# Softmax chain, score-gradient chain and contractions at top priority, and part of the ending moved from VectorE and GpSimd to GpSimd and SyncE

## The chip, the cores and the metric

The kernel runs on one core of one Trainium2 chip. The metric is the device time of one execution in microseconds (us). A core has TensorE (matmuls, "PE" in the profile; its weight loads are "PEld"), VectorE ("DVE"), ScalarE ("ACT"), GpSimd ("POOL") and SyncE ("SP"), which here only issues transfers. The transfers run on 16 DMA engines. Transfers issued by SyncE and by GpSimd stand in two different queues of the profile.

Executions of one kernel spread by 1 to 2% here (the kernel before: 497.7 to 502.1 us in one round of tests, 494.1 to 501.7 in another). A run over 1.5% above the fastest of the same kernel counts as slow and is left out of every ratio.

## The reference

One layer, forward and backward. Two batches, one query each, 32 query heads over 16 heads of keys and values, 4096 keys, head size 128, model size 576, and a bilinear MLP of width 4608:

```python
def _fwd_reference(A_x, A_k_cache, A_v_cache, A_wq, A_wo, B_x, B_w_gate, B_w_up, B_w_down):
    # ... cut: _A_ref is the attention, _B_ref the MLP
    x = A_x
    xn = _layernorm(x, axis=-1)
    return x + _A_ref(xn, A_k_cache, A_v_cache, A_wq, A_wo) + _B_ref(xn, B_w_gate, B_w_up, B_w_down)

def reference(A_x, A_k_cache, A_v_cache, A_wq, A_wo, B_w_gate, B_w_up, B_w_down, B_x, grad_out):
    # ... cut: f is the forward pass of the arguments
    _out, _vjp = jax.vjp(_f, A_x, A_k_cache, A_v_cache, A_wq, A_wo, B_w_gate, B_w_up, B_w_down)
    _grads = _vjp(grad_out)
    return (_out, *_grads)
```

The outputs include the gradients of keys and values, as large as the caches: 92.48 MB are read and 92.48 MB written. There is little arithmetic per byte.

## The kernel before

The attention is cut into 16 steps. A step takes two heads of keys and values of one batch. It transposes K on VectorE and computes scores on TensorE, runs the softmax chain, does the same pass over V for the gradient of the probabilities, and runs the score-gradient chain. The contraction of V with the probabilities (`end_of_V`) closes the step; the contraction of K with the score gradients (`end_of_K`) comes in the next one. The gradients of K and V are outer products: TensorE writes pairs of PSUM banks, ScalarE casts them to bf16, and GpSimd issues stores of 1 MB. Nine of the steps (0, 1, 2, 5, 6, 9, 10, 13, 14) carry a unit of the MLP beside all this.

TensorE, VectorE and ScalarE run their instructions in the order in which the kernel was built. That order is chosen by a scheduler from the written order, from priorities, and from when a buffer can be free.

The two kinds of block that matter below:

```python
    def contract(rowsT, heads):
        o_ps = ps_m([P, Dh])
        with Block() as mm:                     # 64 matmuls, each on 32 of the array's columns
            for c4 in range(4):
                for c8 in range(8):
                    for x, head in enumerate(heads):
                        cg = 2 * x + c8 % 2
                        mm(o_ps[32 * cg:32 * cg + 32, :], lhsT=..., rhs=head[:, 8 * c4 + c8, :], ...)
        # ... cut: copy to SBUF and one small matmul

    def head_scores(n, t, x, s_ps, half):
        # ... cut: one VectorE transposition of a quarter of K or V
        with Block() as mm:                     # 16 matmuls on all 128 columns
            for e in range(2):
                for c8 in range(8):
                    mm(s_ps[:, ...], lhsT=view(X[:], ...), rhs=view(W[t][:], ...), ...)
```

The chain of the softmax, with what each of its small results needs in PSUM:

```python
    def ps_m(shape, dtype=FP32):                # the two "general" PSUM buffers
        return ps.tile(list(shape), dtype, tag="m", bufs=2, name="ps_m")

    def softmax(s_ps):
        s_ps = by_rows(s_ps)
        mx = small("mx")
        nc.vector.reduce_max(mx[:], s_ps[:], axis=AX.X)
        mT = ps_m([1, P])                       # general buffer
        nc.tensor.transpose(mT[:], mx[:], identf[:])
        # ... cut: maximum of mT, then a matmul into a general buffer, then negb on VectorE
        nc.scalar.activation(ex[:], s_ps[:], AF.Exp, bias=negb[:], scale=SCALE, accum_out=z[:])
        z_ps = ps_m([P, 1])                     # general buffer
        # ... cut: probabilities pr, their transposition pT
```

The contractions, the MLP and the small products of the score-gradient chain use the same two general buffers. All banks of PSUM are taken: 2 general, 2 for scores, 2 pairs for outer products, 8 in all.

The main loop and the ending:

```python
    for n in range(NIT):                        # 16 steps
        # ... cut: pass over K, with end_of_K of the step before
        pr, pT, ex, rz = softmax(s_ps)
        prm = masked(pr, "prm")
        # ... cut: pass over V, first part of the next MLP unit
        ds, dsT = dscores(pr, ex, rz, dp_ps)
        dsm = masked(ds, "dsm")
        end_of_V(st, b, s, V, pT)
    # ending: last outer products, gradients of wq and wo of the last group, gradient of x
```

Of the kernel before, what the change touches and what calls it, by code (L numbers as in the profile page):

```python
# [13 lines left out]
P = 128  # L14
# [9 lines left out]
def kernel(  # L24
# [653 lines left out]
    def back_units(st):  # L678
        g, wq, wo, oT = st["g"], st["wq"], st["wo"], st["oT"]
        n0 = g * GH * Dh  # L680
        m = {}
        stq = nat if g == NGRP - 1 else swtile

        def first():
            yp = ps_m([P, 5, 2])
# [25 lines left out]
        def outer_q(k, A):  # L711
            def f():
                R = m["R"]
                if A == 0:
                    m["st"] = stq([P, 2, GH * P], "stq")
                st = m["st"]
                o, whole = ps_pair()
                with Block() as mm:
                    for dc in range(2):
                        for aa in range(2):  # L720
                            a = 2 * A + aa
                            d0 = (2 * k + dc) * P
                            mm(o[aa][:, 256 * dc:256 * dc + 256], lhsT=xnr[32 * a:32 * a + 32, d0:d0 + P],
                                             rhs=R[32 * a:32 * a + 32, 1].rearrange("p h d -> p (h d)"),
                                             start=True, stop=True)
                evac_pair(lambda aa: view(st[:], 0, P, 512 * A + 256 * (aa or 0),
                                          ([[256, 2]] if aa is None else []) + [[GH * P, 2], [1, 256]]), o, whole, 1024,
                          lambda x: x.rearrange("p a (d n) -> p a d n" if whole is not None else "p (d n) -> p d n", d=2))
                if A == 1:
                    nc.gpsimd.dma_start(out_4[256 * k:256 * k + 256, n0:n0 + GH * P].rearrange("(c p) n -> p c n", p=P),  # L730
                                        st[:])
            return f

        def outer_qt():
            R = m["R"]
            st = tailtile("stqt")
            for A in range(2):
                o = ps_o()
                with Block() as mm:
                    for aa in range(2):  # L740
                        a = 2 * A + aa
                        mm(o[64 * A:64 * A + 64, aa, 0:256], lhsT=xnr[32 * a:32 * a + 32, 512:576],
                                         rhs=R[32 * a:32 * a + 32, 1].rearrange("p h d -> p (h d)"), start=True, stop=True)
                evac(st[64 * A:64 * A + 64].rearrange("p (a n) -> p a n", a=2), o[64 * A:64 * A + 64, :, 0:256], 512)
                nc.gpsimd.dma_start(out_4[512:576, n0 + 512 * A:n0 + 512 * A + 512], st[64 * A:64 * A + 64])

        def outer_o(A, h2, k):
            def f():
# [12 lines left out]
                          lambda x: x[:, :, 0:HD2] if whole is not None else x[:, 0:HD2])  # L761
                if h2 == 1 and k == 1:
                    r0 = n0 + 4 * A * P
                    nc.gpsimd.dma_start(out_5[r0:r0 + 4 * P, :].rearrange("(h p) n -> p h n", p=P), m["so"][:])
            return f

        return [[first], [second], [outer_o(0, 0, 0), outer_o(0, 0, 1)], [outer_o(0, 1, 0), outer_o(0, 1, 1)],
# [25 lines left out]
        return n  # L793

    def end_of_K(st, b, s, K, dsT):
        t_ps = contract(dsT, K)
        nc.vector.tensor_scalar(st["oT"][:, 1, 4 * s:4 * s + 4, b], t_ps[:], SCALE, None, op0=ALU.mult)
        dve(0.2)

    def end_of_V(st, b, s, V, pT):  # L800
        t_ps = contract(pT, V)
        nc.vector.tensor_copy(st["oT"][:, 0, 4 * s:4 * s + 4, b], t_ps[:])
        dve(0.2)

# [8 lines left out]
    def final_units():  # L813
# [40 lines left out]
        def gradient():  # L854
            rowf, xn_f, dy_f = m["rowf"], m["xn"], m["dy"]
            dxn = rowf[:, 1, :]
            m1 = fin([2, 1], FP32, "m1")
            nc.vector.reduce_sum(m1[:], dxn, axis=AX.X)
            nc.vector.tensor_scalar(m1[:], m1[:], 1.0 / D, None, op0=ALU.mult)
            xs2 = fin([2, D], FP32, "xs2")  # L860
            m2 = fin([2, 1], FP32, "m2")
            nc.vector.tensor_tensor_reduce(
                out=xs2[:], in0=dxn, in1=xn_f[:], scale=1.0 / D, scalar=0.0,
                op0=ALU.mult, op1=ALU.add, accum_out=m2[:],
            )
            t1 = fin([2, D], FP32, "t1")
            nc.vector.tensor_scalar(t1[:], dxn, m1[:], None, op0=ALU.subtract)
            t3 = fin([2, D], FP32, "t3")
            nc.vector.tensor_scalar(t3[:], xn_f[:], m2[:], None, op0=ALU.mult)
            nc.vector.tensor_sub(t1[:], t1[:], t3[:])  # L870
            nc.vector.tensor_scalar(t1[:], t1[:], rstd[:], None, op0=ALU.mult)
            dx_bf = fin([2, D], BF16, "dx_bf")
            nc.vector.tensor_add(dx_bf[:], t1[:], dy_f[:])
            nc.sync.dma_start(out_1.rearrange("b s d -> (b s) d"), dx_bf[:])

        return [[prepare], [output], [rows], [gradient]]
# [10 lines left out]
    for n in range(NIT):  # L887
# [9 lines left out]
        for x in range(2):  # L897
            K.append(slot(kview, 0, b, l0 + x, s_ps, per, (lambda: end_of_K(*last[:5])) if x == 0 and last else None))
            if x == 0:
# [3 lines left out]
                        side[0:0] = back_units(last[0])  # L903
                        per = -(-len(side) // 4)
                bd1 = build_bd(st, b, s, 1)
        pr, pT, ex, rz = softmax(s_ps)
        prm = masked(pr, "prm")
        if n + 1 < NIT and not new:
            build_W(st, *step(n + 1)[1:], 0)
# [10 lines left out]
                    build_W(nxt, 0, 0, 0)  # L920
        if n + 1 < NIT:
            build_W(nxt if new else st, *step(n + 1)[1:], 1)
        ds, dsT = dscores(pr, ex, rz, dp_ps)
        dsm = masked(ds, "dsm")
        end_of_V(st, b, s, V, pT)
        last = (st, b, s, K, dsT, dsm, bd0)
# [42 lines left out]
```

## Time and profile before

| | before |
|---|---|
| time, median of 3 runs | 500.26 us (498.81 to 502.59) |
| span of the profiled run | 496.4 us |
| moved | 186.06 MB |
| last load landed | 435.5 us |
| from there to the end | 60.9 us |
| last ScalarE cast ended | 489.2 us |

And from the table of stretches, the stretch up to the landing of the last load and the rest (busy us with counts for PE, PEld, DVE, ACT and POOL, then granted TensorE clock, DMA share, GB/s):

```profile
0.00:435.50 435.50, 338.46 (x6671) 235.09 (x6737) 292.28 (x605) 306.46 (x383) 232.13 (x371) 0.91 1.00 391
435.50:496.40 60.90, 40.76 (x675) 22.28 (x680) 34.89 (x76) 41.98 (x57) 31.95 (x34) 0.89 0.71 262
```

While loads still arrive the transfers are always at work and reach 391 GB/s on average; the rest, stores only, goes at 262 GB/s.

### The profile page before, as it was taken

Reading aid. Unit: us, or ns where it says so; the run is one execution under the profiler, and the core shown is the slowest. Engines: PE = TensorE matmul, PEld = TensorE weight load, DVE = VectorE, ACT = ScalarE, POOL = GpSimd, SP = SyncE. Lnnn points to the kernel's source line nnn. Section 1 sums busy time; section 2 is a strip of 40 time slices with the busy share of each in tenths; the row PEclk is TensorE's granted clock in tenths of the full one; section 3 lists DMA queues with packets and bytes.
Section 4 is the critical chain, followed back from the end, with each engine's and each line's share of the span. In section 5 each row is a group of like instructions: output and inputs, shape, how many; then the busy total and the mean of one; then the engine's idle time right before and its main releaser. Section 6 shows DMA issues by size and latency. Waiting matters only on the chain.

```text
span 496.4 us, 16989 instructions
## 1 busy us (share of the span) xinstructions
PE 379.2 (76%) x7344; PEld 257.4 (52%) x7417; DVE 327.2 (66%) x680; ACT 348.4 (70%) x439; POOL 264.1 (53%) x404
## 2 busy tenths in 40 slices
PE   2676887876868877788997768669888869888943
PEld 1655665553645555565665446446556537564510
DVE  6786795861848675855887465666778474884483
ACT  4143877867747857877986768749876777899833
POOL 3245365762634646675546346538647346487613
PEclk9875999988968989989999879969999798999995
DMA  8998999999899999999999999999999999996765
GB/s 256 384 394 304 378 415 390 422 421 407 303 393 356 407 414 360 419 419 412 401 422 407 417 421 346 413 372 353 409 420 411 417 418 372 415 372 240 264 260 190
DMA packets 52899, 186.06 MB, mean 375 GB/s; under 512 B 4140, under 2 KB 19128, under 8 KB 44632
## 3 DMA queue, kind: packets, MB, share of 16 engines
q1 hardware_dynamic: 28392, 92.49, 48.4%
q0 software_dynamic: 24432, 92.48, 47.1%
q8 instruction: 58, 0.95, 0.7%
q14 instruction: 17, 0.14, 0.1%
HBM read 92.48 MB, written 92.48 MB: 373 GB/s over the span
## 4 chain that ended last, share of the span: by engine, by line
DMA 34%; PE 25%; ACT 12%; DVE 11%; issue 7%; POOL 5%; POOLq 0%; ACTq 0%; DVEq 0%
DMA out_dram<-so 22%; PE ps_o L105 10%; ACT so L124 10%; DMA kv<-in_A_k_cache_dram 7%; PE ps_m L105 7%; DVE X L141 6%; DMA kv<-in_A_v_cache_dram 5%; PE ps_sc L105 4%; POOL bd L532 2%; ACT std L124 1%; DVE Xw L141 1%; POOL prm L597 1%; PE ps_m L591 1%; DVE dense L529 1%; ACT sto L124 0%
## 5 line engine op out<-in xcount | busy, mean ns | idle before, releaser
L124 ACT CAST so<-ps_o 128x1024 bf16<-128x1024 f32 x249 | 238.6, 1021 | 70.3 <-PE ps_o L105 29.1
L141 DVE STREAM_TRANSPOSE X<-kv 128x1024 f32<-128x1024 f32 x128 | 157.4, 1232 | 41.2 <-DMA kv<-in_A_k_cache_dram 13.6
L105 PEld LDWEIGHTS <-X 128*128 128x128 bf16 x2048 | 81.9, 103 | 36.6 <-DVE X L141 19.6
L105 PE MATMUL ps_sc<-W,X 128*128 128x64 bf16 (+1 forms) x2048 | 90.1, 200 | 12.1 <-DVE X L141 9.9
L618 POOL DMA_DIRECT2D out_dram<-so x64 | 50.0, 782 | 71.0 <-ACT so L124 43.0
L105 PE MATMUL ps_o<-bd,dsm 128*128 128x512 bf16 x219 | 74.4, 414 | 11.7 <-ACT so L124 8.7
L105 PE MATMUL ps_o<-bd,prm 128*128 128x512 bf16 x212 | 69.0, 396 | 13.8 <-ACT so L124 6.1
L532 POOL TENSOR_TENSOR bd<-dense,maskq 128x1024 bf16<-128x1024 bf16 x32 | 60.6, 1892 | 17.3 <-DVE dense L529 16.1
L124 ACT CAST stw<-ps_o 128x1024 bf16<-128x1024 f32 x36 | 34.4, 1019 | 15.6 <-PE ps_o L105 12.0
L124 ACT CAST std<-ps_o 128x576 bf16<-128x576 f32 x36 | 21.3, 648 | 27.7 <-PE ps_o L105 22.9
L514 POOL COPY W<-rep 32x16 bf16<-32x16 bf16 x128 | 25.0, 195 | 27.0 <-PE ps_sc L105 19.2
L105 PE MATMUL ps_m<-kv,rowT 128*32 128x128 bf16 x2048 | 37.5, 228 | 2.0 <-issue 1.7
L105 PEld LDWEIGHTS <-dsm 128*128 128x128 bf16 x256 | 22.2, 105 | 29.9 <-issue 22.8
L597 POOL TENSOR_TENSOR prm<-pr,maskc 128x1024 bf16<-128x1024 bf16 x16 | 30.2, 1889 | 13.5 <-DVE pr L648 12.8
L105 PEld LDWEIGHTS <-prm 128*128 128x128 bf16 x256 | 21.1, 101 | 28.8 <-issue 15.6
L105 PEld LDWEIGHTS <-rowT 128*32 128x32 bf16 x2048 | 31.1, 101 | 6.9 <-issue 4.4
L597 POOL TENSOR_TENSOR dsm<-ds,maskc 128x1024 bf16<-128x1024 bf16 x16 | 30.4, 1900 | 5.8 <-DVE ds L669 5.5
L124 ACT CAST sto<-ps_o 128x576 bf16<-128x576 f32 x27 | 16.5, 650 | 14.1 <-PE ps_o L105 12.8
L141 DVE STREAM_TRANSPOSE Xw<-wgu 128x1152 f32<-128x1152 f32 x18 | 24.2, 1352 | 2.4 <-PE ps_sc L105 2.4
L105 PEld LDWEIGHTS <-Wdy 128*128 128x128 bf16 x306 | 20.7, 103 | 9.0 <-issue 3.2
L105 PEld LDWEIGHTS <-xnr 32*128 32x128 bf16 (+1 forms) x440 | 13.0, 98 | 19.9 <-issue 15.1
L414 POOL DMA_DIRECT2D out_dram<-stw x18 | 13.9, 771 | 14.4 <-ACT stw L124 14.3
(186 smaller groups left out, 550.5 us busy)
## 6 DMA issues: line engine op xcount, KB each, us to landing
out_dram<-so POOLq DMA_DIRECT2D x64, 1024.0 KB, 13.1
kv<-in_A_k_cache_dram SPq DMA_DIRECT2D x32, 1024.0 KB, 13.0
kv<-in_A_v_cache_dram SPq DMA_DIRECT2D x32, 1024.0 KB, 16.2
out_dram<-stw POOLq DMA_DIRECT2D x18, 512.0 KB, 12.2
wd<-in_B_w_down_dram SPq DMA_DIRECT2D x9, 576.0 KB, 8.1
out_dram<-std POOLq DMA_DIRECT2D x9, 576.0 KB, 10.3
wo<-in_A_wo_dram SPq DMA_DIRECT2D x4, 1152.0 KB, 11.4
wgu<-in_B_w_gate_dram SPq DMA_DIRECT2D x9, 512.0 KB, 14.9
```

What stands on the lines that cost most here:

```text
L105: ins = nc.tensor.matmul(*args, **kwargs)
L124: nc.scalar.copy(out, in_)
L141: nc.vector.transpose(out, in_)
L414: nc.gpsimd.dma_start(out[0:512, f0:f0 + FS].rearrange("(c p) n -> p c n", p=P), st[:])
L514: nc.gpsimd.tensor_copy(view(W[t][:], 32 * a, 32, 48 + 4 * a, [[2 * WW, 4], [WW + 2, 2], [1, 2]]), view(st["rep"][:], 32 * a, 32, t * 4 * ...
L529: nc.vector.tensor_copy(dense[:], bp[:])
L532: nc.gpsimd.tensor_tensor(bd[:], view(dense[:], 0, P, 0, [[Dh, 2], [0, 4], [1, Dh]]), view(maskq[:], 0, P, 0, [[0, 2], [1, 4], [0, Dh]]), ...
L591: nc.tensor.matmul(t_ps[:], lhsT=o_sb[:], rhs=RV[:].rearrange("p x r -> p (x r)"), start=True, stop=True)
L597: nc.gpsimd.tensor_tensor(m[:], view(rows[:], 0, P, 0, [[0, 8], [1, P]]), view(maskc[:], 0, P, 0, [[1, 8], [0, P]]), ALU.mult)
L618: nc.gpsimd.dma_start(oview[b, :, :, l0 + x].rearrange("a m n -> m a n"), st[:].rearrange("p a c d -> p a (c d)"))
```

## The change

It is meant to shorten the way from scores to the next contraction: whatever the chains and contractions need is put before everything else in every engine's order. At the end it takes the last five elementwise steps of the gradient of x off VectorE, which also casts there; on GpSimd they are four. And it lets the idle SyncE issue the last six stores.

```diff
+        store = nc.sync.dma_start if g == NGRP - 1 else nc.gpsimd.dma_start
 # ... the six stores of the gradients of wq and wo: nc.gpsimd.dma_start becomes store
     def end_of_K(st, b, s, K, dsT):
-        t_ps = contract(dsT, K)
+        with tc.high_priority():
+            t_ps = contract(dsT, K)
     def end_of_V(st, b, s, V, pT):
-        t_ps = contract(pT, V)
+        with tc.high_priority():
+            t_ps = contract(pT, V)
 # ... gradient of x
-            nc.vector.tensor_scalar(t1[:], dxn, m1[:], None, op0=ALU.subtract)
+            nc.gpsimd.tensor_scalar(t1[:], dxn, m1[:], rstd[:], op0=ALU.subtract, op1=ALU.mult)
-            nc.vector.tensor_scalar(t3[:], xn_f[:], m2[:], None, op0=ALU.mult)
-            nc.vector.tensor_sub(t1[:], t1[:], t3[:])
-            nc.vector.tensor_scalar(t1[:], t1[:], rstd[:], None, op0=ALU.mult)
+            nc.gpsimd.tensor_scalar(t3[:], xn_f[:], m2[:], rstd[:], op0=ALU.mult, op1=ALU.mult)
+            nc.gpsimd.tensor_sub(t1[:], t1[:], t3[:])
-            nc.vector.tensor_add(dx_bf[:], t1[:], dy_f[:])
+            nc.gpsimd.tensor_add(dx_bf[:], t1[:], dy_f[:])
 # ... main loop
-        pr, pT, ex, rz = softmax(s_ps)
+        with tc.high_priority():
+            pr, pT, ex, rz = softmax(s_ps)
-        ds, dsT = dscores(pr, ex, rz, dp_ps)
+        with tc.high_priority():
+            ds, dsT = dscores(pr, ex, rz, dp_ps)
```

Nothing is computed or moved that was not before.

More of the change, by code (lines that the diff above doesn't have):

```diff
@@ L729, in f @@
                 if A == 1:
-                    nc.gpsimd.dma_start(out_4[256 * k:256 * k + 256, n0:n0 + GH * P].rearrange("(c p) n -> p c n", p=P),
+                    store(out_4[256 * k:256 * k + 256, n0:n0 + GH * P].rearrange("(c p) n -> p c n", p=P),
                                         st[:])
@@ L744, in outer_qt @@
                 evac(st[64 * A:64 * A + 64].rearrange("p (a n) -> p a n", a=2), o[64 * A:64 * A + 64, :, 0:256], 512)
-                nc.gpsimd.dma_start(out_4[512:576, n0 + 512 * A:n0 + 512 * A + 512], st[64 * A:64 * A + 64])
+                store(out_4[512:576, n0 + 512 * A:n0 + 512 * A + 512], st[64 * A:64 * A + 64])
         def outer_o(A, h2, k):
@@ L763, in f @@
                     r0 = n0 + 4 * A * P
-                    nc.gpsimd.dma_start(out_5[r0:r0 + 4 * P, :].rearrange("(h p) n -> p h n", p=P), m["so"][:])
+                    store(out_5[r0:r0 + 4 * P, :].rearrange("(h p) n -> p h n", p=P), m["so"][:])
             return f
```

## The prediction

> **What bounds the kernel now.** I read the page from the slices down, then a table of stretches of the ending, then the ending in order of time. First the busy slices of the page (40 slices of 12.4 us, busy share in tenths):
>
> ```profile
> DVE  6786795861848675855887465666778474884483
> ACT  4143877867747857877986768749876777899833
> DMA  8998999999899999999999999999999999996765
> GB/s 256 384 394 304 378 415 390 422 421 407 303 393 356 407 414 360 419 419 412 401 422 407 417 421 346 413 372 353 409 420 411 417 418 372 415 372 240 264 260 190
> ```
>
> The reader should see two regimes. In slices 2 to 36 (up to about 446 us) the 16 DMA engines are 8 or 9 tenths busy at mostly 400 to 420 GB/s, and no compute engine is full: here the transfers set the pace. In the last four slices (446 to 496 us) the rate falls to 190 to 264 GB/s, so something else sets the pace there. The kernel moves 186.06 MB; at 415 GB/s that would be 448 us, so start, dips and ending together cost 48 us.
>
> The ending by stretches (busy us of each engine, instruction counts in brackets, then granted clock, DMA share and GB/s):
>
> ```profile
> core 0: us, PE busy (x) PEld busy (x) DVE busy (x) ACT busy (x) POOL busy (x), PEclk, DMA share, GB/s
> 428.00:436.00 8.00, 6.52 (x136) 4.51 (x135) 7.52 (x16) 7.07 (x10) 5.70 (x14) 1.00 1.02 415
> ...
> 449.70:457.00 7.30, 5.42 (x35) 2.27 (x36) 1.79 (x5) 7.27 (x8) 4.98 (x6) 1.00 0.59 200
> 457.00:464.00 7.00, 6.18 (x151) 4.04 (x152) 2.95 (x13) 5.98 (x9) 5.82 (x4) 1.00 0.78 295
> 464.00:474.50 10.50, 9.14 (x135) 4.39 (x136) 5.89 (x10) 9.59 (x14) 4.13 (x7) 1.00 0.75 285
> 474.50:484.00 9.50, 3.35 (x21) 1.15 (x21) 8.46 (x20) 1.94 (x5) 0.75 (x1) 0.92 0.65 242
> 484.00:490.30 6.30, 3.72 (x25) 1.08 (x23) 3.95 (x7) 4.13 (x6) 4.02 (x6) 0.50 0.65 229
> 490.30:496.40 6.10, 0.00 (x0) 0.00 (x0) 0.00 (x0) 0.00 (x0) 0.01 (x1) 0.50 0.45 150
> ```
>
> From 449.7 to 474.5 ScalarE is full: 7.27 + 5.98 + 9.59 = 22.84 us of 24.8. Its work there is casting PSUM pairs to bf16 for the stores, 1.02 us for a quarter of a 1 MB tile, so 1 MB per 4.08 us, 257 GB/s: that is the rate of these slices. Then from 474.5 to 484 ScalarE is busy 1.94 of 9.5 us: a hole of 7.6 us, while VectorE is full (8.46). Two things in the order of time make this hole:
>
> ```profile
> 449.73 7.43 ACT L124 CAST so<-ps_o 128x1024 bf16<-128x1024 f32 x8 [0.24 <-PE ps_o L105]
> 449.74 2.29 POOL L826 TENSOR_SCALAR xn_f<-x_f,mu,rstd 2x576 f32<-2x576 f32 x1
> ...
> 450.09 0.08 DVE L635 DVE_READ_ACCUMULATOR2_ANT negb<- 128x1 f32 x1
> ...
> 457.02 0.41 ACT L641 ACTIVATE ex<-ps_sc,negb 128x128 f32<-128x128 f32 x1
> ...
> 457.55 0.29 DVE L661 CUSTOM_DVE_ANT_0 ds<-ex,ps_sc 128x128 bf16<-128x128 f32 x1 [5.92 <-ACT ex L641]
> ...
> 483.31 0.73 DVE L121 CAST sto<-ps_o 128x576 bf16<-128x576 f32 x1
> 483.43 0.39 PE L105 MATMUL ps_x<-dyr,R 32*128 32x288 bf16 x1 [4.41 <-DVE sto L121]
> ...
> 484.10 0.64 ACT L124 CAST sto<-ps_o 128x576 bf16<-128x576 f32 x1 [4.23 <-PE ps_o L105]
> ```
>
> First, the last softmax has its bias `negb` at 450.2, but its exponential stands behind eight casts in ScalarE's queue and runs at 457.0, 6.9 us late; VectorE sits idle 5.92 us for it, and probabilities, contractions, `oT`, and the sums for the gradient of x are all late by it. Second, from 479.97 to 483.0 VectorE does the five elementwise steps of the gradient of x (0.51 + 0.50 + 0.75 + 0.51 + 0.75 us of busy time), with its share of the `sto` casts behind them; TensorE waits 4.41 us for a PSUM buffer that only that cast frees, and ScalarE waits 4.23 us for TensorE.
>
> **What the Trainium skill says.** "TensorE: Matmul & The Clock Gate", section "Architectural detail: the array is 16× 32×32, not 1× 128×128", says ScalarE and VectorE are strict FIFO. The trace agrees: the ready exponential waited 6.9 us behind casts, so its place in the queue is what the priority changes. "GPSIMD Engine Reference", section "3.1 Elementwise — side-by-side cycle accounting", gives 4497 ns against 2293 ns for an fp32 add of 2048 columns, 1.96 times VectorE. The trace has no such add on GpSimd; the subtraction of the same 2x576 shape took 0.75 us on VectorE, so about 1.4 us each is my estimate on GpSimd. The two-scalar form is in the trace: 2.29 us above. "DMA: Bandwidth & Descriptors", section "Latency and other measured facts", gives a first byte after about 0.6 us for SyncE's queue and 1 us for GpSimd's; no run shows that part alone, but issues cost 0.75 us on GpSimd (`sto`) and 0.25 to 0.38 us on SyncE (the small rows, the gate weights). The same page, "Issuing engines are not separate DMA queues", says the transfers share the same 16 engines; the 415 GB/s ceiling with both queues active fits.
>
> **The change, part by part.** I compared the built orders of the two programs engine by engine; they hold no times.
>
> *Priority in the body.* ScalarE's exponentials move ahead of between 0 and 11 casts (counted in casts before each: 69 becomes 63, 204 becomes 196, 295 becomes 284, and so on). TensorE's contractions move ahead of up to about 13 outer-product pairs. VectorE's chain steps move by at most three transposes of keys or values. Busy time is untouched. While DMA share is 0.95 to 1.02 an earlier chain only lets the same bytes go in another order. It can help only in the dips: I asked 5 us stretches and found DMA at 0.61 from 45 to 50 and 0.65 from 130 to 135, some 2 us lost in each, and smaller ones. I allow 1.5 us in all.
>
> *Priority in the ending.* The last exponential goes from 342 casts before it to 330. At the pace of before, ScalarE would reach it near 446.9 and then wait in order for `negb`. On VectorE the chain's order is nearly what it was, so I leave `negb` at 450.2. The chain thus gains 457.0 − 450.3 = 6.7 us, but ScalarE loses about 3 us standing still in front of the exponential. The gain is that `prm`, both contractions, `oT`, the last W products and the accumulation for the gradient come about 6.5 us sooner. In the new order the two `accx` additions and the row copies also stand before casts that they used to follow, and both small GpSimd copies of `Wt` stand before a store rather than behind it. So the 3.15 us that ScalarE waited for TensorE at 474.6 should nearly go.
>
> *The gradient on GpSimd.* VectorE loses 3.0 us between 480.0 and 483.0, so its `sto` casts follow the two reductions directly and the second wait of 4.2 us shrinks to about 1. GpSimd needs 2 × 2.29 + 2 × 1.4 = 7.4 us instead: later by 4.4 us for the gradient itself.
>
> *Stores by SyncE.* Six issues at about 0.35 us instead of 2 × 0.75 + 2 × 0.71 + 2 × 0.56 = 4.0 us on GpSimd: 2 us less issuing. But in SyncE's queue all six stand behind the store of the gradient of x. GpSimd reaches that gradient only after its last 1 MB store. With the reductions done about 5 us earlier than 479.9, thus at about 475, and 7.4 us for GpSimd, the gate opens at about 482.5. The first `sto` will then be ready slightly before and wait; `stq` and `stqt`, ready near 483 to 485, hardly wait.
>
> *Sum for the ending.* ScalarE's idle time from 445 to 489.2 is about 11 us (33 us busy of 44). I take away 3.0 of the first hole, 3.2 of the second and 1 us of small waits; faster chains on idle VectorE bring another 2; and I add 3 us in front of the exponential. That is −3.0 − 3.2 − 1 − 2 + 3 = −6.2: casts then end some 6 us earlier, at about 483. The drain after the last issue was 6.1 us at 150 GB/s. Stores bunched behind the gate (2.3 MB, 5.6 us at 415 GB/s, plus about 2 us) would make it 0.5 us worse, and faster issues take 1.5 us off. Ending: −6.2 − 1.0 = −7.2; with −1.5 for the body −8.7, so 500.3 − 8.7 = 491.6, which I round down to 491 because the body's dips are the less certain term and could give more.
>
> **The rivals.** (1) *The hole is not closed but moved.* ScalarE stands in order before every early exponential; 3 us at the end could be 5, and similar standstills in the body delay casts, leaving a longer backlog when the loads end. For it: ScalarE is full from 449.7 to 474.5. Against it: in the body it is only about 70% busy. That makes 496 to 501. (2) *SyncE becomes the gate.* If the GpSimd chain starts no earlier than 479.9, the gradient lands on the queue at 487.3 and 2.3 MB start only then: about 487.3 + 2 + 5.6 + 1 = 496, no gain from the ending. For it: the built order and 2.29 us per step. Against it: the reductions depend on a chain that is 6.5 us earlier. (3) *The body gains too:* earlier contractions free key and value buffers, whose loads waited 84.8 us in SyncE's queue on the outer products of TensorE, and every dip is filled: up to 5 us more, 484 to 487. Against it: those waits fell while the engines moved 400 GB/s anyway.
>
> **Range and chances.** Ending gains of 3 to 10 us and a body between 2 us worse and 5 us better give 484.5 to 498.5. Two per cent is 10.0 us, thus 490.3, just under my value: 0.44 faster, 0.53 same. A reordering of a body that is limited by transfers can hardly cost 10 us: 0.03.
>
> **What would show it.** Right: the last exponential within 1 us of its `negb`; no hole over 3 us in ScalarE between 474 and the end; VectorE free of gradient steps; the total of body before the last loads land unchanged within 2 us. Wrong: ScalarE idle 5 us or more before the exponential; SyncE's six stores issued in one bunch right after the gradient's store, well after their casts were done; the loads of the last values issued later than the 418 us of now.

## More of the kernel before

A group of matmuls is meant to stay together:

```python
    class Block:                                # ... cut: __init__ and __enter__
        def __call__(self, *args, **kwargs):
            ins = nc.tensor.matmul(*args, **kwargs)
            if self.first is None:
                self.first = ins
                self.stack.enter_context(tc.issue_after(ins.ins))
                self.stack.enter_context(tc.high_priority())
        # ... cut: __exit__ ends both
```

The first matmul has the priority of its place in the program; once it is placed, the others get top priority and so follow it at once.

From the profile's page before: first the busy time of each engine (us, share of the span, instructions); then the chain of work that ended last, as shares of the span.

```profile
PE 379.2 (76%) x7344; PEld 257.4 (52%) x7417; DVE 327.2 (66%) x680; ACT 348.4 (70%) x439; POOL 264.1 (53%) x404
...
DMA 34%; PE 25%; ACT 12%; DVE 11%; issue 7%; POOL 5%; POOLq 0%; ACTq 0%; DVEq 0%
```

Transfers are the largest part of that chain, and TensorE is a quarter of it.

## The result, and the profile after

The changed kernel takes 527.41 us (median of 4, 523.43 to 529.71) beside 501.33 us (498.81 to 502.59) of the kernel before, which had a fourth run by then: a ratio of 1.0518 [1.0436, 1.0601]. A ratio is the mean time of one kernel's fast runs over that of the other's of the same rounds, with its 95% interval, so it is not quite the ratio of the medians. It is 5% slower, 26 us, and the prediction's range ended at 498.5.

The page after, slices first (40 slices of 13.0 us), then busy times and the chain that ended last:

```profile
PE 431.6 (83%) x7417; PEld 280.1 (54%) x7417; DVE 328.5 (63%) x675; ACT 349.9 (67%) x439; POOL 265.9 (51%) x402
...
DMA  7999899998999999999999999998899999647685
GB/s 251 376 399 336 332 404 334 418 421 341 330 417 374 401 351 347 420 379 396 385 411 416 422 404 414 412 365 345 315 374 364 421 333 414 261 182 247 250 321 184
...
PE 44%; DMA 19%; DVE 13%; ACT 9%; POOL 5%; issue 4%; ACTq 0%; DVEq 0%; POOLq 0%
```

VectorE, ScalarE and GpSimd are busy as long as before within 2 us. TensorE is not: 431.6 us against 379.2. (Part of these 52 us is only records: of the outer products of attention 212 and 219 were recorded before and 254 and 250 after, 73 more, which at about 0.4 us each can make up to some 30 us. The run tier below, with as many records as before and no torn block, has 401.5 us: the total alone does not show the tearing.) In the chain that ended last, TensorE and transfers have changed places, from 25 and 34% to 44 and 19%. From the 2nd slice to the 34th the rate was below 380 GB/s in 9 slices before, and is in 16 now.

The stretches up to and from the last load's landing, now at 441.8 us (columns as before):

```profile
0.00:441.80 441.80, 374.13 (x6591) 249.15 (x6592) 289.83 (x589) 293.89 (x366) 225.23 (x358) 0.88 0.98 377
441.80:521.70 79.90, 57.47 (x827) 30.96 (x825) 38.70 (x86) 55.96 (x73) 40.69 (x45) 0.82 0.67 244
```

So 6.3 us are lost before the last load lands and 19.0 after. The second part is a debt of the first: ScalarE had done 293.9 us of its work, mostly casts, by then instead of 306.5, so 19.4 MB of stores were left instead of 15.8, and they leave at 244 GB/s.

The costliest groups of TensorE tell where its extra time is. A row has line, engine, operation, operands, shape, count; then busy us, mean ns of one; then the idle time before them. Before:

```profile
L105 PE MATMUL ps_sc<-W,X 128*128 128x64 bf16 (+1 forms) x2048 | 90.1, 200 | 12.1 <-DVE X L141 9.9
L105 PE MATMUL ps_m<-kv,rowT 128*32 128x128 bf16 x2048 | 37.5, 228 | 2.0 <-issue 1.7
```

After:

```profile
L105 PE MATMUL ps_sc<-W,X 128*128 128x64 bf16 (+1 forms) x2048 | 111.8, 204 | 11.1 <-DVE X L141 8.1
L105 PE MATMUL ps_m<-kv,rowT 128*32 128x128 bf16 x2048 | 60.5, 240 | 2.7 <-issue 2.2
```

Both groups have all 2048 records in both kernels. The mean of one matmul is nearly the same, but the time they cover is not: 23.0 us more for the contractions, 21.7 more for the scores (they overlap each other). Matmuls that used to run close behind one another no longer do. The order in time shows it. A block of scores and a contraction before (start, duration, engine, line, operation, operands, count of a run of like instructions):

```profile
238.22 0.63 PE L105 MATMUL ps_sc<-W,X 128*128 128x64 bf16 x16
...
240.96 0.38 PE L666 MATMUL ps_m<-cs,G 128*128 128x1 f32 x2
241.27 1.08 PE L105 MATMUL ps_m<-kv,rowT 128*32 128x128 bf16 x64
```

And one after:

```profile
221.53 0.25 PE L105 MATMUL ps_sc<-W,X 128*128 128x64 bf16 x3
221.70 0.24 PE L105 MATMUL ps_m<-kv,rowT 128*32 128x128 bf16 x3
221.87 0.20 PE L105 MATMUL ps_sc<-W,X 128*128 128x64 bf16 x1
222.01 0.23 PE L105 MATMUL ps_m<-kv,rowT 128*32 128x128 bf16 x1
222.17 0.20 PE L105 MATMUL ps_sc<-W,X 128*128 128x64 bf16 x1
222.30 0.23 PE L105 MATMUL ps_m<-kv,rowT 128*32 128x128 bf16 x1
...
225.43 0.20 PE L105 MATMUL ps_sc<-W,X 128*128 128x64 bf16 x1
225.56 0.90 PE L105 MATMUL ps_m<-kv,rowT 128*32 128x128 bf16 x49
```

Before, 64 matmuls run in 1.08 us, 0.017 us each: they fill the four groups of 32 columns in turn. After, the block is torn: a contraction matmul, a score matmul, and so on, with 0.29 us from one pair to the next (222.01 to 222.30), or 0.15 us each. The whole block with its 16 scores takes 4.9 us (221.53 to 226.46). A whole block of 16 scores took 0.63 us before, so 1.7 us were needed for both. In the built order of the changed kernel 11 of the 32 contraction blocks are torn in this or a milder way; before, none was. From first to last matmul the 32 blocks add up to 39.3 us before and 69.7 us after.

Who pays for it is in the rows of ScalarE's casts of outer products, before and then after:

```profile
L124 ACT CAST so<-ps_o 128x1024 bf16<-128x1024 f32 x249 | 238.6, 1021 | 70.3 <-PE ps_o L105 29.1
L124 ACT CAST so<-ps_o 128x1024 bf16<-128x1024 f32 x249 | 240.0, 1022 | 95.8 <-PE ps_o L105 69.6
```

ScalarE stood idle 95.8 us before these casts instead of 70.3, and TensorE ended 69.6 us of that instead of 29.1. In the run tier it is 72.8 us idle, 25.1 of them for TensorE. So the late matmuls hold up the casts, and these the stores.

Where the tearing comes from is in the code. A `Block` gives its later matmuls top priority, counted from zero. Inside the contraction's new `with tc.high_priority()` the contraction's matmuls are counted from zero as well. A score block that has begun and a contraction that becomes ready therefore have equal ranks, and the scheduler takes one of each in turn.

The Trainium skill has this in "TensorEngine Tiling (Array Packing)", section "Key Properties": a change of tiling mode, not merely of the tile, drains TensorE. The scores use the array as one piece and the contractions as four strips of 128x32. I had not looked this page up for the prediction. The trace agrees in kind, and supplies the size, about 0.12 us for each switch (0.29 us for a pair, less 0.017 for a contraction matmul and 0.04 for a score in unbroken blocks, halved); the runs do not separate the drain from other costs of alternating.

The skill's "TensorE: Matmul & The Clock Gate", section "Part 3: Packing small matmuls — row/col tiling", says that matmuls start and end in program order. The traces here are in keeping with it (below, a transposition whose input is ready runs 21 us later, behind matmuls of other work), and this makes the second finding possible. Step 14 after, an excerpt of the order in time:

```profile
436.09 0.25 DVE L626 TENSOR_REDUCE mx<-ps_sc 128x1 f32<-128x128 f32 x1
...
451.31 0.67 PE L105 MATMUL ps_m<-hT,wd 128*128 128x2 bf16 x20
...
452.79 1.04 PE L105 MATMUL ps_m<-Xw,Wm 128*32 128x128 bf16 x32
...
457.29 0.27 PE L628 MATMUL ps_m<-identf,mx 128*1 128x128 f32 x1
```

The same step before:

```profile
428.01 0.28 DVE L626 TENSOR_REDUCE mx<-ps_sc 128x1 f32<-128x128 f32 x1
...
431.72 0.27 PE L628 MATMUL ps_m<-identf,mx 128*1 128x128 f32 x1
```

The softmax's row maxima `mx` are ready at 436.3, and their transposition, which has "top priority", runs 21 us later, behind MLP products; before it was under 4. The transposition writes a general PSUM buffer, and so do these MLP products, which come before it in the program. I read the built order thus: the two buffers are given out in program order; top priority moves everything of the chain that needs no such buffer, and the passes over K and V with it, ahead of the MLP unit; the chain's next small result then waits for a buffer that only the MLP unit, now placed last, will free. The urgent work waits for the unhurried one.

### The profile page after: what moved, and what is told of

It reads as the page before. It is cut to its first block, busy times and chain, and to the rows that moved or that the text cites. A ratio compares the mean times of both kernels' runs of the same rounds, so it can differ in the third digit from the quotient of the medians.

```text
span 521.7 us, 17061 instructions
## 1 busy us (share of the span) xinstructions
PE 431.6 (83%) x7417; PEld 280.1 (54%) x7417; DVE 328.5 (63%) x675; ACT 349.9 (67%) x439; POOL 265.9 (51%) x402
## 4 chain that ended last, share of the span: by engine, by line
PE 44%; DMA 19%; DVE 13%; ACT 9%; POOL 5%; issue 4%; ACTq 0%; DVEq 0%; POOLq 0%
PE ps_o L105 17%; PE ps_m L105 13%; DMA out_dram<-so 11%; PE ps_sc L105 9%; ACT so L124 8%; DVE X L141 5%; DMA kv<-in_A_k_cache_dram 4%; DMA out_dram<-stw 4%; POOL bd L532 2%; DVE Xw L141 2%; DVE Xd L141 1%; PE ps_m L591 1%; POOL dsm L597 1%; PE ps_sc L569 1%; PE ps_m L643 1%
## 5 line engine op out<-in xcount | busy, mean ns | idle before, releaser
L124 ACT CAST so<-ps_o 128x1024 bf16<-128x1024 f32 x249 | 240.0, 1022 | 95.8 <-PE ps_o L105 69.6
L105 PE MATMUL ps_sc<-W,X 128*128 128x64 bf16 (+1 forms) x2048 | 111.8, 204 | 11.1 <-DVE X L141 8.1
L105 PEld LDWEIGHTS <-X 128*128 128x128 bf16 x2048 | 93.4, 106 | 42.7 <-DVE X L141 17.6
L105 PE MATMUL ps_o<-bd,prm 128*128 128x512 bf16 x254 | 86.5, 443 | 14.9 <-ACT so L124 10.6
L105 PE MATMUL ps_o<-bd,dsm 128*128 128x512 bf16 x250 | 76.1, 403 | 6.5 <-ACT so L124 5.4
L105 PE MATMUL ps_m<-kv,rowT 128*32 128x128 bf16 x2048 | 60.5, 240 | 2.7 <-issue 2.2
L105 PEld LDWEIGHTS <-rowT 128*32 128x32 bf16 x2048 | 40.6, 106 | 11.6 <-issue 3.1
L105 PEld LDWEIGHTS <-prm 128*128 128x128 bf16 x256 | 22.2, 106 | 35.0 <-issue 24.8
L105 PEld LDWEIGHTS <-dsm 128*128 128x128 bf16 x256 | 20.9, 101 | 26.5 <-issue 17.3
L105 PEld LDWEIGHTS <-Wdy 128*128 128x128 bf16 x306 | 21.5, 106 | 7.9 <-DVE Xo L141 2.9
L105 PEld LDWEIGHTS <-xnr 32*128 32x128 bf16 (+1 forms) x440 | 14.7, 97 | 19.1 <-issue 13.0
## 6 DMA issues: line engine op xcount, KB each, us to landing
out_dram<-so POOLq DMA_DIRECT2D x64, 1024.0 KB, 10.2
out_dram<-stw POOLq DMA_DIRECT2D x18, 512.0 KB, 10.7
wgu<-in_B_w_gate_dram SPq DMA_DIRECT2D x9, 512.0 KB, 15.1
```

Source lines behind the costliest of these rows:

```text
L124: nc.scalar.copy(out, in_)
```

## The experiments

Four theories were put to test. **Torn blocks**: the mixing of contraction and score matmuls costs most of the 26 us. **Chain order**: top priority of the chains in every step is itself harmful, through the general PSUM buffers. **Ending**: the part on GpSimd and SyncE is neutral or harmful, because SyncE's six stores wait for the gradient. **Clock**: the granted clock (0.907 before, 0.871 after) is the cause and not a companion. All kernels below gave correct results. Some of the expectations number their theories: 1 is torn blocks, 2 chain order, 3 the ending; in the second four and in skip, A is the wait for general buffers in steps 10 and 14, and B a cost of early chains as such, through a backlog of stores. "Tier" stands for a priority that ranks after any block that has begun, but before all else: `tc.high_priority(offset=max(0, tc.cur_priority - 1000))`.

### First four: parts alone

**no_contract**: the changed kernel, contractions as before.

```diff
-        with tc.high_priority():
-            t_ps = contract(dsT, K)
+        t_ps = contract(dsT, K)          # and the same for contract(pT, V)
```

> The changed kernel without the priority around the two contractions (both chains, the GpSimd gradient and the SyncE stores stay). In its built order none of the 32 contraction blocks is broken up, against 11 in the changed kernel. Theory 1 (broken contraction blocks are the loss: first-to-last spans of the 32 blocks sum to 69.7 us against 39.3 before): back to 492 to 504 us, sum of spans near 39. Theory 2 (the chains at top priority are the loss, by standing in front of work that could run): still 515 to 527. Theory 3 (the ending: gradient on GpSimd, stores behind it): still above 510.

Measured: 508.09 us beside 499.21, ratio 1.0183 [1.0127, 1.0239]. No block is torn, and the sum of first-to-last times is 38.4 us. So the contraction's priority costs 3.3 points of the 5.2 (a point is 1% of the time before), and 1.8 remain without it. The median lies between the ranges of theories 1 and 2: neither is the whole.

**contract_only**: the kernel before with only the contractions at top priority.

> The kernel before with the priority around the two contractions alone. Built order: 7 of 32 blocks broken up. Theory 1: 512 to 522 us, that is 7/11 or more of the loss of 26 us, and broken blocks of 3 to 5 us in the trace. Theory 2 and theory 3: within 1% of before.

Measured: 509.05 us (502.5 to 511.73), ratio 1.011 [1.0031, 1.0189]. The spread is wide, two of its four runs count as slow and the ratio is of the other two; with all four it would be 508.1 / 499.3 = 1.018. Seven blocks are torn and the sum is 56.7 us. The median lies between the expected ranges. The sign is clear, the size isn't. The profiled run, from which the sum is, was slow, and I draw nothing more from it.

**tail_only**: the kernel before with the gradient on GpSimd and the six stores on SyncE.

> The kernel before with the gradient on GpSimd and the last stores on SyncE alone, no priority changed. Theory 1 and 2: 496 to 501 us (VectorE freed of 3 us in the ending, the stores gated by the gradient). Theory 3: 510 or more.

Measured: 498.47 us, ratio 0.9994 [0.9935, 1.0053]: neutral. The order in time shows why ("SPq" is SyncE's own queue of issues):

```profile
480.40 2.29 POOL L868 TENSOR_SCALAR t<-rowf,m,rstd 2x576 f32<-2x576 f32 x1 [0.26 <-issue]
482.69 0.82 POOL L870 TENSOR_SCALAR t<-xn_f,m,rstd 2x576 f32<-2x576 f32 x1
...
485.06 1.39 POOL L873 TENSOR_TENSOR dx_bf<-t,dy_f 2x576 bf16<-2x576 f32 x1
...
486.06 0.58 ACT L124 CAST stqt<-ps_o 64x512 bf16<-64x512 f32 x1 [0.51 <-PE ps_o L105]
486.47 0.25 SPq L874 DMA_DIRECT2D out_dram<-dx_bf  x1
486.82 0.95 SPq L765 DMA_DIRECT2D out_dram<-sto  x2
487.88 2.40 SPq L731 DMA_DIRECT2D out_dram<-stq  x2
490.37 2.65 SPq L746 DMA_DIRECT2D out_dram<-stqt  x2
```

The last cast ends at 486.6, 2.6 us sooner than before. But all six stores stand behind the store of the gradient of x, which waits for GpSimd until 486.5, and issuing them then takes until 493.0. Before, the last issue had ended at 490.3.

**tier**: the whole change, with every one of its priorities as a tier.

```diff
-        with tc.high_priority():
+        with tc.high_priority(offset=max(0, tc.cur_priority - 1000)):   # in all four places
```

> The changed kernel with all its priorities, but as a second tier: the chains and contractions rank ahead of nearly everything by 1000 places of the program order, yet behind the remaining matmuls of a block that has begun (those rank from place 0). Built order: no contraction block broken, chains still early. Theory 1: 488 to 502 us. Theory 2 (early chains hurt whether or not blocks break): 510 to 527.

Measured: 510.08 us, ratio 1.0233 [1.0181, 1.0286]. No block is torn, the sum is 38.0 us. Against 1.0518 the same priorities without tearing are 2.85 points better, 14 us of 499. What stays, 2.3 points, has nothing to do with torn blocks: the median is just inside the range that theory 2 gave and 8 us above that of theory 1, so tearing is the larger part of the loss, not all of it.

### Second four: which chain, and why

**softmax_only**: the changed kernel with priority on the softmax chain alone (ending kept). **dscores_only**: the same with the score-gradient chain alone.

```diff
-        with tc.high_priority():
-            ds, dsT = dscores(pr, ex, rz, dp_ps)
+        ds, dsT = dscores(pr, ex, rz, dp_ps)      # softmax_only; both contractions plain too
```

> The changed kernel with priority on the softmax chain alone (no contraction, no chain of the score gradients). In its built order the first TensorE step of the softmax in steps 10 and 14 stands behind the MLP unit and the pass over V, as in the run without contraction priority. Theory A: 505 to 512 us, the whole loss of the chains. Theory B: about half of it, 502 to 506.

> The changed kernel with priority on the chain of the score gradients alone. Its built order in steps 10 and 14 is that of before. Theory A: 496 to 502 us. Theory B: about half the loss, 502 to 506.

Measured: softmax_only 507.73 us, 1.0175 [1.0105, 1.0245]; dscores_only 499.77 us, 1.0018 [0.9964, 1.0071]. The softmax chain carries all that no_contract had lost. The time from the chain's first instruction to the transposition of its maxima, in steps 10 and 14 (from the traces, us):

| kernel | step 10 | step 14 | ratio |
|---|---|---|---|
| before | 5.4 | 5.5 | 1 |
| dscores_only | 7.0 | 7.2 | 1.0018 |
| softmax_only | 21.3 | 21.1 | 1.0175 |
| no_contract | 18.5 | 21.5 | 1.0183 |
| skip (below) | 5.8 | 5.9 | 1.0043 |
| tier | 7.8 | 23.8 | 1.0233 |
| own_slots_tier (below) | 2.0 | 2.7 | 1.0086 |
| after | 16.1 | 22.6 | 1.0518 |

The wait does not grow in every step: from the row maxima to their transposition, step 9 went from 10.8 us before to 4.1 in no_contract and step 13 from 7.6 to 2.3. And tier, late in step 14 above all, loses no less than softmax_only.

**own_slots_tier**: the tier kernel, with the chains' four small results no longer in general buffers but in unused columns of the score tile's bank. **own_slots_before**: its control, the kernel before with only that move.

```diff
-        s_ps = ps_sc()
-        nc.tensor.transpose(s_ps[:], s_sb[:], identf[:])
+        s_ps = ps.tile([P, 512], FP32, tag="sc", bufs=2, name="ps_sc")
+        nc.tensor.transpose(s_ps[:, 0:P], s_sb[:], identf[:])
-        mT = ps_m([1, P])
+        mT = s_ps[0:1, P:2 * P]           # the other three likewise
```

> The second-tier kernel (510.08 us, nothing broken, chains at top) with the chains' small PSUM results (maximum, its spread, sum, row term) in unused columns of the score tile's bank, so that they no longer share the two general PSUM buffers with the MLP unit. Theory A (slots: in steps 10 and 14 the first TensorE step of the softmax stands behind the MLP unit's products and the whole pass over V, 21.5 to 23.8 us after its scores against 5.5 before, because its PSUM buffer comes third in line): 485 to 500 us, and that step within 8 us in step 14. Theory B (backlog: earlier chains let loads run ahead of stores, 18.8 MB still to store at the last load's landing against 15.8): still 504 to 512.

> The kernel before with the chains' small PSUM results in the score tile's bank, no priority changed: the control of the run beside it. Theory A: 495 to 501 us, little changed, since before the chain was late by 4 us at most in step 14. Theory B: the same.

Measured: 503.06 us, 1.0086 [1.0036, 1.0137]; the control 501.54 us, 1.0049 [0.9976, 1.0122]. Freed from the general buffers the tier kernel takes 7 us less (510.08 to 503.06; the intervals do not overlap), and the difference to its control is within noise. Step 14's wait is gone, as theory A had it, but 503.06 lies between A's range and B's: the buffers carry about 1.5 of the 2.3 points, and a remainder may be the backlog. (An earlier form with a PSUM buffer of its own for the chains didn't build, as all 8 banks are in use.)

### Third four: repairs

**contract_tier**: the kernel before with the contractions as a tier, nothing else.

```diff
-        t_ps = contract(pT, V)
+        with tc.high_priority(offset=max(0, tc.cur_priority - 1000)):
+            t_ps = contract(pT, V)        # and contract(dsT, K)
```

> The kernel before with the two contractions alone ahead of nearly everything, but as a second tier behind the rest of a begun block: in the built order all 32 blocks are whole, against 7 torn in the run with plain priority (1.011 of before in fast runs). Torn blocks are the loss: 0.99 to 1.003 of before. Early contractions are the loss: 1.008 or more.

Measured: 496.51 us beside 500.11, ratio 0.9952 [0.9902, 1.0002]. The same early contractions that cost over 1% when they tear cost nothing when they don't. This pair, beside after and tier, is what the first finding rests on.

**ungated** (5 rounds): tail_only, with the store of the gradient of x issued last.

```diff
-            nc.sync.dma_start(out_1.rearrange("b s d -> (b s) d"), dx_bf[:])
+            kept.append(dx_bf)
+    with tc.issue_after(tails[-1].ins):   # after the last weight store on SyncE
+        nc.sync.dma_start(out_1.rearrange("b s d -> (b s) d"), kept[0][:])
```

> The run with the changed ending alone (0.9994 of before), with the store of the gradient of x issued last in SyncE's queue instead of ahead of the six weight stores. If SyncE's queue was the gate that ate what VectorE gained: 2 to 4 us less than before, 495 to 497. If nothing was gained by freeing VectorE: within 1 us of before.

Measured: 494.94 us, ratio 0.9918 [0.9881, 0.9955]. SyncE's issues in order of time:

```profile
481.93 1.54 SPq L766 DMA_DIRECT2D out_dram<-sto  x2
...
485.00 1.11 SPq L732 DMA_DIRECT2D out_dram<-stq  x2
...
486.20 2.57 SPq L747 DMA_DIRECT2D out_dram<-stqt  x2
488.87 0.40 SPq L941 DMA_DIRECT2D out_dram<-dx_bf  x1
```

The first store goes at 481.9 instead of 486.8, and the last issue ends at 489.3 instead of 493.0. The gate was worth about 0.8% of the time.

**only15_ungated** (5 rounds): ungated, with top priority for both chains in the last step only.

```diff
-        pr, pT, ex, rz = softmax(s_ps)
+        with (tc.high_priority() if n == 15 else ExitStack()):
+            pr, pT, ex, rz = softmax(s_ps)    # and dscores
```

> The same, with both chains at top priority in the last step alone (the last exponential stands 8 to 12 casts earlier; all blocks whole; orders of earlier steps unchanged). My prediction's account of the ending would make this 4 to 8 us faster than before, 491 to 495. If ScalarE is full anyway and only the order of its casts changes: like the run beside it.

Measured: 492.73 us, ratio 0.9853 [0.9811, 0.9896], 7 us better than before (one of its six runs, 500.67 us, counts as slow and is left out). Beside ungated this tests the prediction's main term. The last exponential in this trace:

```profile
452.47 0.37 ACT L642 ACTIVATE ex<-ps_sc,negb 128x128 f32<-128x128 f32 x1
```

It was at 457.02 before: 4.6 us earlier, in a run whose last load landed 1.4 us later. The casts end at 487.0 (489.2 before). Beyond ungated the gain is 0.65 points, and the two intervals overlap. That the 7 us in all equal the 7.2 that the prediction gave to the ending is luck: about half of them come from removing the gate, which it had counted as nearly free.

**gradient_only**: the kernel before with the gradient on GpSimd, stores left on GpSimd.

> The kernel before with the gradient of x on GpSimd alone; the last stores stay on GpSimd, which issues them after its four gradient steps. In-order GpSimd then delays them by some 7 us against the end of the reductions: 1 to 4 us slower than before if that gate counts, within 1 us if the drain hides it.

Measured: 500.8 us, ratio 1.0025 [0.9974, 1.0076]: no gain. Freeing VectorE alone is worth nothing here; it gained only where the stores also left GpSimd and did not wait for the gradient (ungated). Ungated stores on SyncE with the gradient left on VectorE were not run, so how ungated's gain divides is open.

### Last three: the chain's steps, the remainder, a combination

**skip**: no_contract with chain priority off in steps 9, 10, 13 and 14, so on in 12 of 16 steps.

```diff
-        with tc.high_priority():
+        with (tc.high_priority() if n not in (9, 10, 13, 14) else ExitStack()):
```

> The changed kernel without contraction priority (1.0183 of before), and with the chains' priority left off in steps 9, 10, 13 and 14 only; in its built order the softmax's first TensorE step of steps 10 and 14 stands where before has it, amid the pass over V. The other 12 steps keep the priority. Theory A (late first step behind the MLP unit in steps 10 and 14): 0.992 to 1.004 of before. Theory B (early chains in general): about 12/16 of the loss, 1.012 or more.

Measured: 501.5 us, ratio 1.0043 [0.9971, 1.0116]. The trace of step 14, to be set beside no_contract's. no_contract:

```profile
418.69 0.25 DVE L626 TENSOR_REDUCE mx<-ps_sc 128x1 f32<-128x128 f32 x1
...
438.83 0.27 PE L628 MATMUL ps_m<-identf,mx 128*1 128x128 f32 x1 [0.23 <-DVE accx L323]
```

skip:

```profile
430.57 0.28 DVE L626 TENSOR_REDUCE mx<-ps_sc 128x1 f32<-128x128 f32 x1
...
434.71 0.32 PE L628 MATMUL ps_m<-identf,mx 128*1 128x128 f32 x1
```

Leaving four steps alone takes back 1.4 of the 1.8 points (theory A expected at most 1.004, B at least 1.012). With it the maxima come 12 us later than in no_contract, and their transposition 4 us earlier. One of its runs, the profiled one, had a granted clock of 0.713 and took 502.76 us; the other three took 496.15 to 503.21 us. TensorE was busy 415.8 us in that run. So neither a lower clock nor a busier TensorE makes 26 us by itself, and the clock theory is out.

**own_tier_ungated**: own_slots_tier with the ungated ending.

> The kernel with all priorities as a second tier and own PSUM columns for the chains (1.0086 of before), with the store of the gradient of x moved behind the weight stores. If the rest of its loss is SyncE's gate in the ending: 0.8% less, 0.997 to 1.003. If it is something of the early chains themselves: 1.005 or more.

Measured: 498.25 us, ratio 1.0004 [0.9944, 1.0065]. The change as intended, with its three faults mended (tearing, general buffers, gate), is as fast as the kernel before, no faster; it stands 0.86 points behind ungated, which has the same ending and no priorities (their intervals just overlap).

**best** (5 rounds): only15_ungated with the contractions as a tier.

> What helped, together: contractions as a second tier in all steps (0.9952 alone), chains at top priority in the last step only, ending with the gradient on GpSimd and its store last on SyncE (0.9853 together). If the gains add: 0.978 to 0.984. If the earlier contractions only feed the loads, which then wait for the same stores: 0.983 to 0.990.

Measured: 492.56 us, ratio 0.99 [0.9843, 0.9958]. It is the same as only15_ungated within noise; the gains of contract_tier and only15_ungated don't add.

## Why the prediction was wrong

**The sum of the change.** In points of the time before (1 point is 5 us), each with the runs that it is a difference of:

| part | from | points |
|---|---|---|
| torn contraction blocks | after against tier | +2.85 |
| softmax chain at top priority in every step | softmax_only against tail_only | +1.8 |
| contractions early beside early chains, not torn | tier against no_contract | +0.5, intervals overlap |
| score-gradient chain | dscores_only against tail_only | +0.2, within noise |
| ending as changed | tail_only | −0.1, within noise |

These make 5.25 points; the changed kernel has 5.18. This is less of a test than it looks: the first and third rows together are after less no_contract by construction. Only the other three are tested, 1.9 points together against the 1.83 of no_contract, and with runs of different rounds and intervals of about half a point or more each that close fit is partly luck.

**The step that failed: "Busy time is untouched."** The prediction had the built orders and noted that contractions "move ahead of up to about 13 outer-product pairs". It counted how far a block moves, and did not look at whether the block was still whole. What a block takes depends on the order: the same 64 contraction matmuls covered 1.08 us or, with 16 scores among them, 4.9. The slices that the prediction shows leave TensorE out, too, though the page has it at 9 tenths in 5 of 40 and at 25% of the chain that ended last. That is 2.85 of the 5.2 points. The nearest thing that it wrote, that contractions pass outer products, names the wrong neighbour: the damage was done by score matmuls.

**The second step that failed: "While DMA share is 0.95 to 1.02 an earlier chain only lets the same bytes go in another order", and from it "can hardly cost 10 us".** The first half is true, but another order is not free. In no_contract the last load landed at 427.4 us instead of 435.5, so the loads did get ahead. But 18.7 MB of stores were left then instead of 15.8, and the rest took 76.8 us instead of 60.9. After has 19.4 MB and 79.9 us. What is passed over in the body comes due in the ending, where casts set the pace (the prediction itself read 257 GB/s from 1.02 us per cast) against 391 GB/s in the body. At the 262 GB/s of the ending before, 1 MB takes 3.82 us, at the body's 391 GB/s 2.56; moving 2.9 MB from one to the other costs by my estimate 2.9 × (3.82 − 2.56) = 3.7 us; the rest of no_contract's 9 us I put down to the wait behind the MLP unit in steps 10 and 14. Skip fits this but does not prove it, as it takes away both at once: its last load landed at 436.3, with 16.4 MB left. That the general buffers are the reason for the wait rests on own_slots_tier (7 us back, with about as much left to store as after) and on the built order; a kernel that moves only the MLP's buffers was not run.

**The ending, first term: the exponential 6.7 us earlier.** The mechanism was right. Even in the changed kernel the last exponential ran within about 0.3 us of its bias, 4.4 us after its scores against 11.7 before; only all of that was some 17 us later on the clock (474.33 against 457.02). Where nothing else is changed (only15_ungated) it came 4.6 us earlier. ScalarE did not stand still for 3 us in front of it, as the sum had it: in the changed kernel casts run without a listed gap up to 474.33, and in only15_ungated the cast before it ended at 452.57. But its worth was overstated: 0.65 points beyond ungated, about 3 us. By my reading ScalarE's casts were the queue either way.

**The ending, second and third term: VectorE freed, SyncE's issues.** VectorE lost its gradient steps, and the wait of 4.2 us became 1.25 us or less (1.14 in the changed kernel). GpSimd's gradient took 2.29 + 0.82 + 1.39 + 1.39 = 5.9 us and not 7.4: the second two-scalar step was cheaper. The "about 1.4 us" for an addition was right, with some luck: the ratio 1.96 of "GPSIMD Engine Reference", section "3.1 Elementwise — side-by-side cycle accounting", times 0.75 us gives 1.47, and the ratio here was 1.85. "Six issues at about 0.35 us" was mis-sized: 0.95 + 2.40 + 2.65 = 6.0 us in tail_only, more than the 4.0 us that it replaced. The size had been read from SyncE's shortest issues; in the trace before, 31 of its 131 took over 1 us and the longest 10.2. Rival 2, SyncE as the gate, is what happened. Its "If the GpSimd chain starts no earlier than 479.9" came true at 480.40, and its 496 us is what tail_only gave: 498.47 as median and 496.5 as span. I had given it too little weight because I built the ending on the exponential. Rival 3 hoped that loads would wait less: their waits for TensorE's outer products fell from 84.8 us to 43.1, but those for its matmuls into the general buffers, mostly contractions, rose from 36.2 to 101.8. (Two slips of the working: its ranges for ending and body give 485.3 to 499.3, not 484.5 to 498.5, and its last exponential moves by 12 casts, not by at most 11. Neither matters beside 527.)

**By its own signs.** Signs of being right: "the last exponential within 1 us of its `negb`": yes. "no hole over 3 us in ScalarE between 474 and the end": yes, the longest listed is 1.29 us. "VectorE free of gradient steps": yes. "the total of body before the last loads land unchanged within 2 us": no, 6.3 us later. Signs of being wrong: ScalarE idle for 5 us before the exponential: no. "SyncE's six stores issued in one bunch right after the gradient's store": yes, from 512.0 to 518.2, with the store of the gradient at 511.7; the casts of four of the six were over by 510.8, the last one at 511.9. "the loads of the last values issued later than the 418 us of now": yes, the last at 427.9. Three of four signs of being right came true, and the value was still off by 36 us: these three all looked at the ending, and the loss was made by the order of the body, even where it came due later.

**What stays open.** Why an early chain that neither tears nor waits for general buffers gains nothing (own_tier_ungated, 1.0004), though its last load lands at 418.0, 17 us sooner than before: the ending of 77.4 us is the cast-paced debt by my reading. It had 3.8 MB more to store at that point than before, 4.8 us by the estimate above, and it is 4 us slower than ungated; but moving the small results alone may cost 0.5 points (own_slots_before, within noise), and no run gave the ending faster casts. And how contract_only's 1.1 to 1.8 points divide.

## What to carry to other kernels

Raising a priority moves an instruction only as far as its buffers allow: look for what of the passed-over work holds the buffer that the urgent work needs next. After any change of priorities count in the built order whether blocks of matmuls that belong together still follow one another, above all where narrow and full-width matmuls share TensorE; priorities of the same rank interleave. And where a kernel is paced by transfers in its body and by one engine at its end, ask of each reordering what it postpones, not only what it brings forward.

## What the Trainium skill lacked or had wrong

- "TensorEngine Tiling (Array Packing)", section "Key Properties", says that a change of mode drains TensorE, but gives no size. Here alternating 128x32 and full-width matmuls, whatever the drain's share, took 0.29 us a pair, against 0.017 us for each contraction matmul in an unbroken block (64 in 1.08 us) and 0.04 us for each score matmul (16 in 0.63 us).
- "DMA: Bandwidth & Descriptors", section "Issuing engines are not separate DMA queues", calls the time to initiate a transfer "usually small relative to the DMA itself". For SyncE at the end of tail_only it was 1.05 to 1.34 us for each of four stores issued close together (2.40 and 2.65 us for two), where two of them took 5.4 us from issue to landing; against 0.71 and 0.56 us for the same stores from GpSimd in the kernel before, and 0.25 us for the one store ahead of them. No run shows what the longer issues wait for.
- "GPSIMD Engine Reference", section "3.1 Elementwise — side-by-side cycle accounting", has the two-input addition (here 1.39 us for 2x576, 1.85 times VectorE's 0.75, 6% under its ratio of 1.96). It has no figure for an operation with two per-partition scalars. I used the trace alone, and that misled: 2.29 us for the first of two of the same shape and 0.82 us for the second directly behind it.
